# A new instruction order for an S4 block with an MLP: the MLP's first four column blocks computed in two halves of the tokens

## The chip, the core and the metric

The kernel runs on one core of a Trainium2 chip. The core has five engines that run on their own and meet through semaphores: TensorE (PE; its weight loads are shown apart as PEld), VectorE (DVE), ScalarE (ACT), GpSimd (POOL) and SyncE (SP), which only issues DMAs here. Matrix products land in PSUM, eight banks per partition; everything else lies in SBUF. The metric is the device time of one execution in microseconds, as the median over runs.

## What is computed

The input x has 2048 tokens of 512 channels (bf16). First a state-space convolution is added to it, then an MLP:

```python
h  = x + A(layernorm(x))          # y = irfft(rfft(u) * rfft(K)) + u * Dskip, per channel, 2048 taps
h2 = h + B(layernorm(h))          # B: layernorm, gelu(y @ w1 + b1) @ w2 + b2; w1 is 512 x 1376
# the taps, from 128 complex modes per channel:
K[d, l] = Re( sum_n C[d,n] * exp(dt[d] * A[d,n] * l) * dt[d] * B[d,n] )
# l is rounded to bf16 before the exponential
```

## The kernel before

The convolution is done with a Fourier transform of 4096 points split into two factors, on PE. Channels are handled in four groups c = 0 to 3 of 128; tokens in two halves b = 0 and 1, each of two quarters sb. The stages, with the lines that do them:

1. Loads and small tables. The decay th = dt * A_re comes from an exponential on ACT, a transpose on PE and one DVE product (L791). From it ACT makes exponentials (`bexps`, L795 and L798; `aexps`, L1016). Other DVE work builds phases (`split`, `wrap`, `restack`). A table load (`table`, L557) switches ACT from exponentials to sines.
2. `chain` (four calls): PE adds phases in PSUM (L1062, L1068), ACT takes sine and cosine (L1072), DVE multiplies them with the exponentials (L1039, L1079 to L1090). In the calls of kind "B" the sine table is negated in place (L1080, "sign pass") between two uses.
3. `kgen` (per channel group): 512 small matmuls in two lines (L1113, L1114) give the taps of a group; ACT or DVE casts them out of PSUM (`evac`: L563 on ACT, L565 on DVE), and a small DVE addition (L1127) puts in Dskip. `carry` (L1134) shifts rows with four DMAs of SP.
4. `kspec` (L1157), a write to DRAM (`AK_d`) and a read back turn the layout; `fstage` (L989) finishes the kernel's spectrum. This is done for each pair of channel groups q and each block.
5. `xspec` (L969) and `fstage` do the same for the input, after layer norm (`ustats`, `stats`, `unorm`).
6. `inverse` (per b and c): DVE or GpSimd multiplies spectra (L1205, L1210, L1213), PE transforms back (L1221), `evac` casts, and a transposing DMA of SP (`turn`, L1227) puts tokens on partitions.
7. `lead` and `tail`: adding the convolution to x, statistics, a reciprocal root on GpSimd (`root`, L925), scale and shift (L1340 on ACT or L1338 on DVE), and the transpose of the normalized tokens, on PE for the first quarter (L1349, cast at L1351) and by `turn` for the others.
8. `mlp` (per quarter): 11 column blocks of w1, four matmuls of 512 tokens each (L1369), gelu on ACT (L1371), and the second product (L1391) with the addition of h on DVE (L1393) and the store.

Nothing is scheduled while the kernel runs. Each `add` call makes one operation and numbers it, in program order, from 0 to 969. The list ORDER, written out in the file, is the order in which the operations are emitted, and each engine does its own in that order. A negative entry ~n means operation n on the second engine of those that it allows. `Sched.run` walks the list with planned costs and arrival times; the plan decides which of four PSUM tiles of two banks an operation gets (`slots`) and where PE gets filling matmuls (L1485) in planned gaps. Operations of GpSimd wait for the DVE operation that stands before them in the list ("turns").

Operations that matter below, by their numbers in the old list:

| numbers | what |
|---|---|
| 15; 16 to 18 | bit fields: GpSimd's memsets; three DVE operations on them (L695 to L697) |
| 47, 48 | th and its negative copy |
| 76 to 79 | two DVE sums and their squares on ACT |
| 108, 116 | the scaled copies of `split` |
| 545 to 552 | statistics of the input's second half (L945) |
| 418 to 433; 434 | `kgen` of groups 2 and 3; its last cast |
| 436 to 439; 440, 443 | `carry` and `kspec` for groups 2 and 3, first block |
| 446, 447; 448, 449 | writes of that spectrum to DRAM; reads back |
| 408, 409 | reads of the second block of groups 0 and 1 |
| 450 to 457; 469 to 476 | `fstage` and casts, first and second block of groups 2 and 3 |
| 534, 538, 541; 542, 543 | last products of the first half's inverse; its last transform and cast |
| 544 | the `turn` of it |
| 575 to 608 | parts of `xspec(1)` and their casts |
| 609 to 615 | loads of w1 (four, 344 KB each), w2 (two of 640 KB, one of 96 KB) |
| 639; 640 | `root` of the first quarter; scale and shift from it |
| 641, 643, 646, 648 | the normalizations of the first quarter's four token tiles |
| 645, 650 | the casts of the two halves of its transpose |
| 674 to 694 | the MLP's column blocks of the first quarter (even numbers PE, odd ones ACT; 694 is the last) |
| 727 to 776; 777 | products of the second half's inverse; its last transform |

Of the kernel before, what the change touches and what calls it, by code (L numbers as in the profile page):

```python
# [162 lines left out]
class VS(V):  # L163
# [91 lines left out]
class Ring:  # L255
# [12 lines left out]
    def until(self, t0):  # L268
        o = 0.0
        for a, b in self.q:  # L270
            o += max(0.0, min(b, t0 + 5.0) - max(a, t0))
        return t0 + 3.3 + 0.4 * min(o, 5.0)


class Sched:
# [40 lines left out]
    def run(self, nslots):  # L316
# [13 lines left out]
        for code in ORDER:  # L330
# [46 lines left out]
            if e == "PE":  # L377
# [4 lines left out]
                while n0 < ipe:  # L382
# [3 lines left out]
                    if (n1 - 193) % 256 == 0:  # L386
                        t = blk = max(t, ring.until(blk))
# [39 lines left out]
def c_dve(n, mode=1, psum=False):  # L427
    return (0.09 if n < 64 else 0.065) + (0.07 if psum and n > 700 else 0) + n / mode / 960.0
# [1098 lines left out]
```

## Time and profile before

| | us |
|---|---|
| median of three runs | 240.29 (240.02 to 241.02) |
| the profiled execution | 238.53 |
| its span, first to last instruction | 236.8 |
| PE busy | 203.2 (86%) |
| DVE busy | 176.7 (75%) |
| ACT busy | 172.2 (73%) |
| GpSimd busy | 46.0 (19%) |
| mean granted clock of PE | 0.990 |

Times in the profile count from the first instruction. Busy time says little here, since the stages have different limits: a stage is read by which engine is nearly full in it, and by the chain of waits, which goes back from the last instruction to what released it each time. "issue" in that chain is time in which the engine waited for nothing that the profile shows. L12 is line 12 of the kernel. A group's time may be a helper's: all casts have L563 or L565.

### The profile page before, as it was taken

What the parts mean: (1) busy time and instruction counts of PE and PEld (TensorE: products, weight loads), DVE (VectorE), ACT (ScalarE), POOL (GpSimd) and SP (SyncE); (2) the same over time, 40 slices, a digit from 0 to 9 for tenths busy, and PEclk for the clock granted to TensorE, in tenths of its full rate; (3) what the DMA queues carried; (4) which work ended last, traced back from release to release, by engine and by line L of the source; (5) the groups of instructions that cost most, each with busy time, mean ns of one, the idle gap of its engine ahead of it and who ended that gap; (6) DMA issues with size and microseconds to landing.
All of it is one profiled execution on the core that took longest, in us unless ns stands there. A gap on an engine that the chain in (4) does not pass through costs nothing.

```text
span 236.8 us, 7706 instructions
## 1 busy us (share of the span) xinstructions
PE 203.2 (86%) x3285; PEld 114.0 (48%) x3285; DVE 176.7 (75%) x323; ACT 172.2 (73%) x210; POOL 46.0 (19%) x224
## 2 busy tenths in 40 slices
PE   3219686768999999998979888999999999999994
PEld 2203432324875387865657544544444444444443
DVE  3999997999999975678979999988954757222022
ACT  5999999899899996696979959989456305604700
POOL 5945760000000140319400001520000101000000
PEclk9999999997999999999999999999999999999998
DMA  5692210200000549534897797470654051421212
GB/s 172 145 202 60 60 36 0 48 2 3 6 3 10 136 126 278 200 93 143 250 233 160 174 220 202 112 178 24 121 110 83 0 111 44 91 55 48 51 33 55
DMA packets 42293, 24.15 MB, mean 102 GB/s; under 512 B 25810, under 2 KB 39604, under 8 KB 42260
## 3 DMA queue, kind: packets, MB, share of 16 engines
q1 hardware_dynamic: 41810, 23.34, 41.2%
q8 instruction: 25, 0.41, 0.7%
q10 hardware_dynamic: 450, 0.33, 0.6%
q14 instruction: 8, 0.07, 0.1%
HBM read 9.90 MB, written 6.29 MB: 68 GB/s over the span
## 4 chain that ended last, share of the span: by engine, by line
PE 53%; ACT 24%; DMA 8%; DVE 7%; issue 5%; SPq 1%; POOL 1%; DVEq 0%; ACTq 0%; POOLq 0%
PE ps L1369 16%; PE ps L1391 13%; ACT ar L798 6%; ACT ar L563 6%; PE ps L1114 4%; PE ps L1113 4%; ACT ar L1072 4%; ACT ar L1016 4%; DMA ar<-ar 4%; PE ps L1068 3%; PE ps L969 3%; DMA ar<-AK_d 3%; PE ps L989 2%; ACT ar L647 2%; PE ps L1157 2%
## 5 line engine op out<-in xcount | busy, mean ns | idle before, releaser
L563 ACT CAST ar<-ps 128x1024 bf16<-128x1024 f32 (+4 forms) x72 | 65.1, 970 | 16.7 <-PE ps L1287 2.8
L1371 ACT ACTIVATE ar<-ps,ar 128x512 bf16<-128x512 f32 (+1 forms) x44 | 28.8, 688 | 30.9 <-PE ps L1369 29.7
L1369 PE MATMUL ps<-ar 128*128 128x512 bf16 (+1 forms) x176 | 40.2, 379 | 0.3 <-ACT ar L563 0.3
L1391 PE MATMUL ps<-ar 128*128 128x512 bf16 (+3 forms) x187 | 39.9, 367 | 0.0
L1072 ACT ACTIVATE ar<-ps 128x1024 bf16<-128x1024 int16 x36 | 34.7, 1049 | 1.9 <-PE ps L1068 1.6
L1393 DVE TENSOR_TENSOR ar<-ps,ar 128x512 bf16<-128x512 f32 (+1 forms) x17 | 11.2, 658 | 28.9 <-PE ps L1391 24.2
L565 DVE CAST ar<-ps 128x1024 bf16<-128x1024 f32 (+1 forms) x20 | 23.3, 1185 | 8.8 <-PE ps L1114 3.7
L1205 DVE TENSOR_TENSOR ar<-ar 128x2048 bf16<-128x2048 bf16 x21 | 25.2, 1220 | 3.6 <-PE ps L1221 3.3
L1391 PEld LDWEIGHTS <-ar 128*128 128x128 bf16 (+1 forms) x187 | 17.9, 98 | 19.8 <-issue 0.4
L1369 PEld LDWEIGHTS <-ar 128*128 128x128 bf16 (+1 forms) x176 | 17.3, 100 | 20.6 <-issue 1.1
L1068 PE MATMUL ps<-ar 128*32 128x512 f16 (+1 forms) x368 | 21.8, 346 | 5.6 <-ACT ar L1072 5.6
L1485 PE MATMUL ps<-ar 128*128 128x512 bf16 x57 | 15.7, 412 | 9.3 <-DMA ar<-in_A_u_dram 7.2
L1114 PE MATMUL ps<-ar 128*20 128x33 bf16 x512 | 20.9, 249 | 1.2 <-issue 1.2
L1113 PE MATMUL ps<-ar 128*20 128x33 bf16 x512 | 20.7, 248 | 0.5 <-issue 0.4
L925 POOL TENSOR_TENSOR ar<-ar 128x4 f32<-128x4 f32 (+1 forms) x5 | 5.7, 1148 | 77.8 <-DVE ar L614 51.5
L1113 PEld LDWEIGHTS <-ar 128*20 128x20 bf16 x512 | 18.5, 124 | 2.2 <-issue 1.3
L989 PE MATMUL ps<-ar 128*32 128x256 bf16 (+1 forms) x384 | 18.9, 310 | 0.6 <-DMA ar<-AK_d 0.3
L1114 PEld LDWEIGHTS <-ar 128*20 128x20 bf16 x512 | 18.3, 125 | 2.1 <-issue 1.7
L1068 PEld LDWEIGHTS <-ar 128*32 128x32 f16 x368 | 10.3, 101 | 15.2 <-issue 12.4
L969 PE MATMUL ps<-ar 128*32 128x512 bf16 x256 | 17.0, 380 | 0.6 <-issue 0.5
L1039 DVE TENSOR_TENSOR ar<-ar 128x2048 bf16<-128x2048 bf16 x14 | 16.5, 1212 | 0.0
L624 DVE TENSOR_TENSOR ar<-ar 128x4 f32<-128x4 f32 (+8 forms) x38 | 12.9, 352 | 3.7 <-POOL ar L693 2.8
(113 smaller groups left out, 289.4 us busy)
## 6 DMA issues: line engine op xcount, KB each, us to landing
AK_d<-ar SPq DMA_DIRECT2D x8, 512.0 KB
ar<-AK_d SPq DMA_DIRECT2D x8, 512.0 KB
ar<-in_A_u_dram SPq DMA_DIRECT2D x4, 512.0 KB
out_dram<-ar SPq DMA_DIRECT2D x30, 64.0 KB
ar<-in_B_w_dram SPq DMA_DIRECT2D x4, 344.0 KB
ar<-ar SPq DMA_DIRECT2D x20, 64.0 KB
ar<-in_B_w_dram SPq DMA_DIRECT2D x2, 640.0 KB
ar<-ar SPq DMA_DIRECT2D x8, 48.0 KB
```

The source lines that it names most:

```text
L563: act.copy(out_fn(), in_fn())
L565: dve.tensor_copy(out_fn(), in_fn())
L969: pe.matmul(pst(p)[32 * cg:32 * cg + 32, 512 * z:512 * z + 512], lhsT=BD.ap()[:, 32 * f + 2 - 2 * jl:32 * f + 34 - 2 * jl], rhs=un[2 * (2 ...
L989: pe.matmul(pst(p)[64 * h + z:64 * h + z + 32, w * (k + r):w * (k + r) + w], lhsT=T.ap()[:, f, r, z:z + 32], rhs=rhs(f), start=True, stop= ...
L1068: pe.matmul(pst(p)[32 * g:32 * g + 32, 256 * j:256 * (j + n)].rearrange("p (a b) -> p a b", a=n), lhsT=W2[DELTAS.index(d)].ap(), rhs=S2[g] ...
L1072: add("ACT", c_act(1024), lambda e, o_=o_, i_=i_: act.activation(o_(), i_(), ACT.Sin, scale=SINSC), r=[p, TBL], w=[sc[cs]])
L1113: pe.matmul(o, lhsT=Ar.ap()[:, :, d], rhs=Br.ap()[:, :, d], start=True, stop=False, tile_position=(0, 32 * g))
L1114: pe.matmul(o, lhsT=Ai.ap()[:, :, d], rhs=Bi.ap()[:, :, d], start=False, stop=True, tile_position=(0, 32 * g))
L1205: (dve if e == "DVE" else gp).tensor_tensor(pieces(o).rearrange("p z (a r d) -> p a z r d", a=4, r=2), k, x, ALU.mult)
L1369: pe.matmul(pst(p)[:fs, 512 * z:512 * z + 512], lhsT=w1s[dc].ap()[:, fc * P:fc * P + fs], rhs=ybuf.ap().rearrange("p (t c) k -> p c t k", ...
L1371: add("ACT", c_act(512, 1), lambda e, p=p, z=z, fc=fc, fs=fs: act.activation(hT.ap()[:fs, fc, :], pst(p)[:fs, 512 * z:512 * z + 512], ACT. ...
L1391: pe.matmul(pst(p)[:, 512 * z + c0:512 * z + c1], lhsT=hT.ap()[:fs, fc, 128 * t:128 * t + 128], rhs=w2s[fc].ap()[:fs, c0:c1], start=(fc == ...
```

## The change

There are four parts.

- `mlp`: for the first quarter of the tokens and the first four column blocks, the four matmuls over 512 tokens become two operations of four matmuls over 256 tokens each. The first reads only the first half of the transposed input. This makes four operations more, 974 in all; numbers above 674 shift by up to four in the new file. The text goes on with the old numbers.
- The sign pass may be put on GpSimd by the list, and its instruction has two constants, -1 and 1.
- ORDER is another list. Operations change their place in every queue, and some fifty their engine.
- The planner's constants differ: when PE's instructions are refilled (`Ring.until`, 192 for 193), the costs of the first loads, of transposes on PE.
- Nothing else changes: the same products, tables and transfers.

```diff
@@ ORDER (beginning, and the stretch from the first casts to the MLP)
-    163, -204, 0, 81, 1, 11, 12, 43, 44, 15, 132, 16, 17, 18, 2, 45, 5, 162, 3, 131, 6, 161, 66, 4, 14, 13, 46, 47, 50, 48, 62, 34, 19, 8, 60, 54, 28,
...
+    43, -27, 81, -287, 82, 131, 12, 0, 44, 1, 11, 46, -204, 4, 14, 2, 38, 132, 15, 3, 67, 45, 47, 13, 48, 5, 16, 17, 68, 66, 49, 18, 50, 87, 69, 163,
...
+    276, 418, 419, 420, 423, 386, 503, 545, 421, 546, 383, 504, 402, 547, 548, 403, 422, 549, 404, 161, 424, 425, 550, 551, 552, 553, 554, 427, 428,
+    483, 501, 405, 502, 406, 484, 507, 555, 508, 556, 426, 429, 430, 558, 557, 432, 433, 485, 505, 559, -280, 388, 560, 561, -279, -432, 387, -563,
...
+    490, 511, 396, 611, 491, 439, 578, 579, 580, 438, 437, 436, 443, -513, 444, 446, 509, 498, 499, 510, -446, 615, 409, 397, 398, -501, 572, 573,
+    574, -619, 280, 599, 600, 515, -517, 524, 590, 591, 592, 518, 519, 520, 416, 417, 527, 408, 412, 410, 411, 569, 570, -572, 413, 525, 528, 529,
+    521, 447, -726, 448, 450, 449, 452, -527, -452, 595, 522, 453, -597, 610, 456, 457, 454, 455, 575, 531, 576, 534, 577, 538, 458, 532, 535, 460,
+    533, 530, 597, 541, 536, 593, 598, -595, 523, 724, 726, 727, 539, 540, 542, 543, 739, 459, 414, 415, 584, 537, 585, 587, 588, 589, 619, 620, 623,
+    728, 729, 624, 730, -587, -733, 461, 462, 621, 622, 626, 464, 625, 463, 544, 651, 627, 652, 654, 628, 629, 653, 603, 604, 631, 630, 581, 582, 583,
+    632, 634, 605, 612, 465, 633, 606, 656, 635, 636, 659, 637, 601, 466, 638, 639, 602, 607, 608, 655, 657, 640, -647, -642, -644, 609, 642, 658,
...
@@ Ring
     def until(self, t0):
         o = 0.0
         for a, b in self.q:
-            o += max(0.0, min(b, t0 + 5.0) - max(a, t0))
-        return t0 + 3.3 + 0.4 * min(o, 5.0)
+            o += max(0.0, min(b, t0 + 5.5) - max(a, t0))
+        return t0 + 3.65 + 0.3 * min(o, 5.5)
@@ chain
-                add("DVE", c_dve(1024, 4), lambda e, sc=sc: dve.tensor_scalar(sc[0].ap(), sc[0].ap(), -1.0, None, ALU.mult), r=[sc[0]], w=[sc[0]])
+                add(("DVE", "POOL"), (c_dve(1024, 4), 0.92), lambda e, sc=sc: (dve if e == "DVE" else gp).tensor_scalar(sc[0].ap(), sc[0].ap(), -1.0, 1.0, ALU.mult, ALU.mult), r=[sc[0]], w=[sc[0]], hv=9)
@@ mlp
-                def fn(e, p=p, z=z, fc=fc, fs=fs):
-                    for dc in range(4):
-                        pe.matmul(pst(p)[:fs, 512 * z:512 * z + 512], lhsT=w1s[dc].ap()[:, fc * P:fc * P + fs], rhs=ybuf.ap().rearrange("p (t c) k -> p c t k", c=4)[:, dc], start=(dc == 0), stop=(dc == 3))
-                add("PE", 0.87, fn, r=[ybuf] + w1s, w=[p], new=[p] if z == 0 else [], hv=1)
+                for t0, t1 in ((0, 2), (2, 4)) if b + sb == 0 and fc < 4 else ((0, 4),):
+                    def fn(e, p=p, z=z, fc=fc, fs=fs, t0=t0, t1=t1):
+                        for dc in range(4):
+                            pe.matmul(pst(p)[:fs, 512 * z + 128 * t0:512 * z + 128 * t1], lhsT=w1s[dc].ap()[:, fc * P:fc * P + fs], rhs=ybuf.ap().rearrange("p (t c) k -> p c t k", c=4)[:, dc, t0:t1], start=(dc == 0), stop=(dc == 3))
+                    add("PE", 0.2175 * (t1 - t0), fn, r=[ybuf[4 * t0:4 * t1]] + w1s, w=[p], new=[p] if z == 0 and t0 == 0 else [], hv=1)
```

More of the change, by code (lines that the diff above doesn't have):

```diff
@@ L382, in run @@
                 while n0 < ipe:
-                    n1 = min(ipe, n0 - (n0 - 193) % 256 + 256)
+                    n1 = min(ipe, n0 - (n0 - 192) % 256 + 256)
                     t = clk.work(t, c * (n1 - n0) / o.ni, o.act / o.cost[0])
                     n0 = n1
-                    if (n1 - 193) % 256 == 0:
+                    if (n1 - 192) % 256 == 0:
                         t = blk = max(t, ring.until(blk))
@@ L655 @@
     tE(bf16, 512)
-    dma("ACT", lambda: ldt.ap(), lambda: A_log_dt.rearrange("(o d) -> o d", o=1), 1024, [], [ldt], pr=0, cost=0.42)
+    dma("ACT", lambda: ldt.ap(), lambda: A_log_dt.rearrange("(o d) -> o d", o=1), 1024, [], [ldt], pr=0, cost=-0.28)
     for n, (nm, ap) in enumerate((("are", A_A_re), ("cre", A_C_re), ("cim", A_C_im), ("bre", A_B_re), ("bim", A_B_im), ("aim", A_A_im))):
         raw[nm] = tE(bf16, 4, P)
-        dma(("SP", "ACT", "SP", "ACT", "SP", "SP")[n], lambda v=raw[nm]: v.ap(), lambda a=ap: a.rearrange("(p dt) n -> p dt n", dt=4), 131072, [], [raw[nm]], pr=0.01 * n, cost=0.42)
+        dma(("SP", "ACT", "SP", "ACT", "SP", "SP")[n], lambda v=raw[nm]: v.ap(), lambda a=ap: a.rearrange("(p dt) n -> p dt n", dt=4), 131072, [], [raw[nm]], pr=0.01 * n, cost=(0.0, 0.05, 0.42, 0.05, 0.42, 0.42)[n], k=1.25)
     xv = x_dram.rearrange("(b q j h l) d -> b h q j (l d)", b=2, j=4, h=2, l=2)
@@ L785, in fn @@
                 pe.transpose(pst(p, bf16)[:, 128 * d:128 * d + 128], raw[nm].ap()[:, d, :], identb.ap())
-        add("PE", 0.6, fn, r=[raw[nm], identb], w=[p], new=[p])
+        add("PE", 0.3, fn, r=[raw[nm], identb], w=[p], new=[p])
         return p, (lambda: nat(pst(p, bf16)[:, 0:512]))
@@ L812, in trf @@
                 pe.transpose(pst(p, bf16)[:, 512 * n + 128 * d:512 * n + 128 * d + 128], raw[nm].ap()[:, d, :], identb.ap())
-        add("PE", 0.6, trf, r=[raw[nm], identb], w=[p], new=[p] if n == 0 else [])
+        add("PE", 0.27, trf, r=[raw[nm], identb], w=[p], new=[p] if n == 0 else [])
         pas.append(lambda p=p, n=n: nat(pst(p, bf16)[:, 512 * n:512 * n + 512]))
```

57 rows, old and new, of the table ORDER are left out of this document.

## The prediction

> **What bounds the kernel now.** I first read the span, the bandwidth in 40 slices of 5.9 us, and a table of busy times by stage (columns: length, then PE, its weight loads, DVE, ACT and GpSimd, each with its number of instructions; granted clock; busy share of the DMA engines; GB/s), with stages cut where the chain of waits changes hands.
>
> ```profile
> span 236.8 us, 7706 instructions
> ...
> GB/s 172 145 202 60 60 36 0 48 2 3 6 3 10 136 126 278 200 93 143 250 233 160 174 220 202 112 178 24 121 110 83 0 111 44 91 55 48 51 33 55
> ...
> 36.30:83.60 47.30, 39.74 (x1019) 23.63 (x1017) 45.86 (x92) 44.05 (x52) 0.80 (x3) 0.96 0.12 26
> 83.70:101.90 18.20, 16.78 (x661) 14.16 (x657) 10.90 (x18) 13.37 (x14) 4.31 (x4) 1.00 0.62 196
> 101.90:120.70 18.80, 17.89 (x413) 11.11 (x403) 17.02 (x17) 16.70 (x19) 9.37 (x4) 1.00 0.67 188
> 120.70:135.40 14.70, 12.66 (x313) 8.96 (x313) 12.84 (x13) 12.97 (x14) 0.00 (x0) 1.00 0.87 164
> 135.40:150.00 14.60, 13.02 (x145) 6.67 (x145) 13.58 (x29) 10.99 (x15) 1.03 (x1) 1.00 0.94 229
> 150.00:173.50 23.50, 23.44 (x187) 10.95 (x186) 22.10 (x37) 17.28 (x24) 5.08 (x2) 1.00 0.47 102
> ...
> 195.20:236.80 41.60, 38.06 (x188) 18.27 (x185) 11.72 (x26) 14.47 (x22) 1.01 (x1) 0.98 0.23 54
> ```
>
> From 36 to 84 us DVE is busy for 45.86 of 47.30 us; from 84 to 102 PE is (16.78 of 18.20), from 102 to 150 nobody alone, and from 150 on PE is busy throughout. So the end is the time at which the MLP's PE work begins, plus what PE still has to do, plus its waits. Then the chain of waits (start, length, what), in order of time.
>
> ```profile
> 4.02 0.18 DVE ar L624
> ...
> 4.78 0.64 DVE ar L624
> 5.44 0.63 ACT ar L795
> 6.07 8.52 ACT ar L798 x9
> 14.59 1.04 ACT ar L647 x2
> ...
> 18.14 0.52 ACT ar L632
> ...
> 23.15 0.52 ACT ar L632
> ...
> 34.54 1.28 ACT L557
> ...
> 88.08 0.43 PE ps L989 x8
> ...
> 101.96 0.51 DVE ar L565
> ...
> 114.65 6.03 DMA ar<-AK_d
> ...
> 122.72 1.24 issue
> ...
> 128.81 4.74 ACT ar L563 x5
> ...
> 135.40 5.46 DMA ar<-ar
> ...
> 142.48 1.30 ACT ar L563 x2
> ...
> 145.93 2.21 ACT ar L1340 x3
> 148.14 0.51 ACT ar L563
> ...
> 148.94 1.02 ACT ar L563
> 150.00 1.94 PE ps L1369 x8
> ...
> 172.75 0.77 DVE ar L1213 x2
> 173.56 0.56 PE ps L1221 x14
> ...
> 195.21 9.50 PE ps L1369 x44
> ```
>
> The reader should see five hand-overs: a late start of ACT (5.44); PE until the kernel of the last channels is out (101.96); a round trip through DRAM until 120.68; ACT's casts until 135.4; the transposing DMA, statistics and normalization until 150.0. Last, the grouping by line gives prices (busy, mean ns of one, idle before):
>
> ```profile
> L1205 DVE TENSOR_TENSOR ar<-ar 128x2048 bf16<-128x2048 bf16 x21 | 25.2, 1220 | 3.6 <-PE ps L1221 3.3 <-ACT ar L563 0.2
> ...
> L1205 POOL TENSOR_TENSOR ar<-ar 128x2048 bf16<-128x2048 bf16 x3 | 12.2, 4069 | 13.3 <-DMA ar<-ar 8.2 <-ACT ar L563 5.1
> ...
> L945 DVE BATCH_NORM_STATS2 ar<-ar 128x6 f32<-128x512 bf16 x16 | 9.7, 670 | 0.0
> ...
> L1080 DVE TENSOR_SCALAR ar<-ar 128x1024 bf16<-128x1024 bf16 x8 | 3.3, 426 | 0.0
> ...
> L1434 DVE TENSOR_SCALAR ar<-ar 128x1024 bf16<-128x1024 bf16 x1 | 0.4, 443 | 0.0
> ```
>
> **The change part by part.** Numbers of operations are those of the old list. The planner's new constants move no operation of the list; they set only how many filling matmuls (L1485) are put into planned gaps of PE, which wait for nothing and are costed at 0, and which PSUM tile an operation gets.
>
> *The sign pass* (L1080) gets a second engine, but no negative entry of the new list names one of its eight operations: it stays on DVE. Its new two-constant form is that of L1434, 443 ns against 426: 8 x 0.02 = +0.1, taken as 0.
>
> *The split* adds 16 matmuls and 16 weight loads. Only one half block (674, first half) stands in the new list ahead of work that needs both halves of the transposed input: after it come 732, then 694 with all tokens. That is 0.43 us of PE work (two matmuls' worth at 9.50/44 = 0.216) and the 0.47 of 732, in the gap between the two casts at 148.14 and 148.94, where the old list had 469 and 471 (2 x 0.43). So I take 0 (ends: -0.4, and +0.4 if weight loads show between short matmuls).
>
> *The order* is the rest. Step 1: the first product (47, row 4.78) stood behind three field operations that waited for GpSimd (4.02 on). Now 47 and 48 stand first. The timeline has 47's two inputs, the exponential and the transpose:
>
> ```profile
> 2.65 0.60 ACT L647 ACTIVATE ar<-ps 128x512 bf16<-128x512 f32 x1
> ...
> 2.94 0.61 PE L785 MATMUL ps<-ar 128*128 128x128 bf16 x4 [0.33 <-DMA ar<-in_A_A_re_dram]
> ```
>
> Both were ready at 3.6, so 47 starts at 3.7 and ACT 1.0 earlier. GpSimd's identity, now behind five memsets of DVE (some 0.7 us), is hidden by the load that this transpose waits for. Step 2: two scaled copies (rows 18.14, 23.15) leave ACT for DVE, 2 x 0.52 = -1.0. But ACT now reaches the squares (row 14.59) at 4.4 + 2 x 0.52 + 7 x 0.947 (8.52/9) = 12.1, and DVE has their inputs at some 13.6 only, one earlier than before: +1.0. Together -1.0 at the table load (34.54).
>
> Step 3, the DVE stage to 83.6: eight statistics (545 to 552; 9.7/16 = 0.6 each from start to start) go behind it, -4.8 with what hangs on them -5.7, and 3.9 of small work, most of it from GpSimd, comes in. The last product would be 2.8 earlier with step 1. But PE now does one kernel-spectrum group and four input groups ahead of 418, which the old list had behind, and gets there at some 83. I take -1.0 for 418 (ends 0, -2.8).
>
> Step 4, PE to 101.96: ten groups of eight matmuls leave the stretch up to 433, at 0.43 each (row 88.08): -4.3. Their casts have room (ACT 13.37 and DVE 10.90 of 18.20). The last kernel cast is 5.3 earlier, at 96.7.
>
> Step 5, the round trip (carry, spectrum, write 447, read 448 and 449; 18.7 us in the rows from 101.96 to 120.68). SP's timeline has the writes 446 and 447 (start, length from the first issue to the end of the last):
>
> ```profile
> 106.59 4.30 SPq L575 DMA_DIRECT2D AK_d<-ar  x2
> ```
>
> SP's queue now has 615 (96 KB) and the reads 409 and 408 (512 KB each) between 446 (512 KB) and 447. That is 1.6 MB ahead of 447, 6.5 us at 250 GB/s (the fastest slices from 89 to 124 us show 278, 250 and 233), of which 4.3 pass before 447 is issued anyway: +2.2. Arrival at 117.6, 3.1 earlier.
>
> Step 6, arrival to the last cast of the first inverse (543), 14.7 us: ACT has nine casts left after the first PE group (457, 455, 577, 460, 533, 536, 598, 540, 543), 0.7 + 9 x 0.95 (4.74/5) = 9.2, where thirteen and three waits stood. DVE's three products behind the second of them end earlier than that. So -5.5: 543 ends at 126.8, 8.6 earlier.
>
> Step 7, to the MLP: the transposing DMA (5.46) and the statistics stay. ACT then has five postponed casts (604, 583, 606, 602, 608) before the first normalization, 0.4 + 4.7 us from the last lead cast's start, where 3.4 passed (142.48 to 145.93): +1.7. One normalization more on ACT is balanced by PE starting on the first of two casts. GpSimd's root (639) stands behind a 4.07 us product, which starts eight DVE operations earlier. The weights 609 are moved from 90.5 to behind write 466, whose casts stand ten casts ahead of 650 on ACT; a load of 344 KB lands in that time. So far 6.9 earlier, 143.1.
>
> How tight is that? From 83.7 to 150.0 ACT is busy 13.37 + 16.70 + 12.97 + 10.99 = 54.0 of 66.3 us, idle 12.3. The new list gives ACT 2.0 more in that stretch (counted at 0.9 a cast) and the steps make it 5.8 shorter: 4.5 idle of 60. Its densest stage above has 44.05 of 47.30, the same share. I give back 1.1, the ends being 0 and all 6.9: the MLP begins at 144.2, and the scale and shift that release the normalizations (640) are 5.8 earlier.
>
> Step 8, after the MLP began. PE has 1.8 more to do (469, 471, 732, 740 follow instead of preceding). DVE has more, too: four products' worth of the second half (727, 729, 736, 737 and four small ones, 5.9) came behind 640, four tail operations (2.4) went ahead, and one product comes from GpSimd (1.1; another went there earlier): +4.3 net of a normalization. DVE's timeline has 640 at
>
> ```profile
> 145.57 0.16 DVE L640 SCALAR_TENSOR_TENSOR ar<-ar 128x4 f32<-128x4 f32 x1
> ```
>
> From there to the last product (172.75 + 0.77 = 173.52) DVE took 27.9; now 32.2, from 139.8 to 172.0. PE comes to that inverse (777) after 25.0 us (48 matmuls of L1369 and 44 of L1391 at 0.216 take 19.9, six inverse groups at 0.56 3.4, four spectrum groups at 0.43 1.7), at 169.2, and waits 2.9. Its work from there on is 0.65 shorter. The end moves by (172.1 - 173.56) - 0.65 = -2.1 us. Most of the early gain is given back here.
>
> The profiled execution took 238.53 us for a span of 236.8, 1.8 below the median of 240.29; a difference of spans is put on the median: 238.2.
>
> In the Trainium skill, Runtime: NRT & Kernel Launch, section Instruction fetch mechanics, refills of 256 instructions are called mostly hidden. Its rule prices the 32 added PE instructions at nothing, which is the sum above. The row 122.72 disagrees, if that wait is a refill: PE waited 1.24 us for nothing that the profile shows while DMA was 0.87 busy. With one more such wait the sum would be 239.4.
>
> **The rivals.** *No change*: DVE decides. If 640 comes only 3.7 earlier, step 8 returns all of it: -3.7 + 4.3 - 0.65 = 0, 240.3. For it: 22.10 of 23.50 us busy on DVE after 150. Against: 1.4 idle there may also close.
>
> *Slower*: the round trip of step 5. The stage 120.7 to 135.4 moved 164 GB/s at 0.87 busy; at that rate the 1.6 MB take 9.9 us, 3.4 later, and the end is +1.3: there it decides. At 150 GB/s it is +4.4 on the arrival, +2.3, 242.6. For it: 408 and 409 now fall into the trip; before, 447 had the queue to itself. Against: the stage 135.4 to 150.0 moved 229.
>
> *The order doesn't bring the MLP forward*: a list is matched to planned durations, and what is gained up to 433 goes into waits between five queues in fixed order. With 640 where it was, step 8 alone is left: +4.3 - 0.65 = +3.6, 243.9. For it: idle time of 4.5 us in 60 is little for ACT. Against: ten groups out of the stretch that PE bounds is a count and no plan.
>
> **How the numbers follow.** Forecast -2.1: 0.53, from 234.6 (-2.1, less the 1.1 given back, step 3's other 1.8 and half of DVE's 1.4 idle) to 239.1. No change, 239.1 to 241.5: 0.20. Slower by the round trip, 241.5 to 243.5: 0.17; by an MLP that isn't earlier, 242 to 245: 0.10. The range leaves out about 0.1 on each side: 234.5 to 243.0. 0.5% is 1.2 us, about what a measurement can tell. So faster 0.53, same 0.20, slower 0.27.
>
> **What would show it.** Steps 1 and 2: first L795 at 4.4, second table load at 33.5. Step 4: the last L1127 at 97. Step 5: the first inverse group after the read at 118. Step 7: first L1369 near 144. Step 8: PE idle before one L1221 group, released by L1213, near 170. I am wrong if the read lands after 121, if L1369 starts after 147, or if PE does not wait there at all (then faster still).

## The result, and the profile after

The changed kernel is slower: 242.19 us median (240.08 to 243.02) against 240.02 us of the kernel before, measured beside it; ratio 1.0124, 95% interval 1.0078 to 1.0171. The forecast was 238.2 us, faster. The same kernel was timed three more times beside the experiments, on three chips, at ratios of 1.0048 (1.0005 to 1.0090), 1.0062 (1.0018 to 1.0106) and 1.0039 (0.9998 to 1.0080). So it loses 0.4 to 1.2%, and the sign of the forecast was wrong. The profiled execution after took 240.91 us for a span of 239.1, before 238.53 for 236.8. Line numbers of the changed kernel are one higher than before up to L1367, two higher behind the MLP's matmul, which was L1369 and is L1371.

First the page's span of the changed kernel and its table of busy times by stage, cut where the same operations end that cut the table before (columns as there).

```profile
span 239.1 us, 7770 instructions
...
82.20:100.40 18.20, 14.70 (x594) 12.10 (x596) 9.12 (x21) 11.75 (x12) 1.92 (x3) 0.91 0.51 155
100.40:121.40 21.00, 19.87 (x473) 12.38 (x464) 17.85 (x21) 18.49 (x20) 10.00 (x5) 1.00 0.73 203
121.40:131.30 9.90, 9.62 (x244) 6.59 (x245) 9.27 (x9) 8.83 (x10) 0.35 (x1) 1.00 1.15 153
131.30:148.40 17.10, 16.30 (x184) 7.46 (x182) 14.91 (x33) 16.15 (x21) 5.10 (x2) 1.00 0.85 237
148.40:176.10 27.70, 26.78 (x270) 14.59 (x273) 26.16 (x38) 20.18 (x27) 1.01 (x1) 1.00 0.47 101
```

The kernel stage (first row, from 418 to 433) begins 1.5 us earlier and has 2.1 us less PE work than before (14.70 for 16.78), and yet it is as long (18.20). Its mean granted clock is 0.91, where it was 1.00. The stage behind it (the DRAM round trip) is 2.2 longer, the next one 4.8 shorter, the one to the MLP 2.5 longer. Then the chain of waits (start, length, what), first three rows of the kernel before, then the changed kernel.

```profile
88.89 0.36 issue
...
96.71 0.55 issue
...
224.58 8.69 PE ps L1391 x51
```

```profile
90.08 1.82 issue
...
96.98 1.39 issue
...
107.12 1.03 PE ps L1158 x16
108.25 1.24 DVE ar L566
109.53 6.04 DMA AK_d<-ar
115.95 5.48 DMA ar<-AK_d
121.47 0.65 PE ps L990 x16
...
131.67 1.02 ACT ar L564
...
148.44 0.60 PE ps L1371 x4
...
226.94 8.69 PE ps L1393 x51
```

The reader should see two things. Two waits for nothing that the profile shows, 1.82 and 1.39 us, stand in the kernel stage, where the longest was 0.55 before. And the MLP begins at 148.44, 1.6 earlier than before, but the last PE row ends at 235.63, where it ended at 224.58 + 8.69 = 233.27. So 3.9 us are lost behind the MLP's beginning. Most of it is PE's own work, as the busy times from there to PE's end show (columns as above), before and after:

```profile
150.00:233.27 83.27, 83.14 (x491) 38.90 (x490) 45.35 (x87) 40.72 (x58) 7.09 (x4) 1.00 0.33 70
```

```profile
148.44:235.63 87.19, 86.10 (x567) 41.95 (x572) 48.56 (x87) 43.80 (x62) 3.02 (x3) 1.00 0.34 72
```

PE is busy 3.0 us longer (0.4 of it two filling matmuls) and idle 1.0 us longer. DVE's timeline has the two ends that the forecast used for this part, the scale and shift (640) and the last product of the second half's inverse (776, second of the two in its row).

```profile
143.75 0.16 DVE L641 SCALAR_TENSOR_TENSOR ar<-ar 128x4 f32<-128x4 f32 x1
...
175.18 0.76 DVE L1214 TENSOR_TENSOR ar<-ar 128x512 bf16<-128x512 bf16 x2
```

From 143.75 to 175.94 it is 32.2 us. Before it was 27.9, and 32.2 was forecast.

The milestones of the runs that follow, read from the traces (us; 433 is the last kernel matmul group, 447 the last spectrum write, 456 the first group of `fstage` after the read, 543 the last cast of the first inverse; "MLP" is the first MLP matmul, "rest" the time from it to PE's end):

```
run              433 ends  447 issued  456 starts  543 ends  640    MLP     rest
before            101.9      110.5       120.7      135.4   145.6  150.0    83.3
changed           100.4      109.5       121.5      131.2   143.8  148.4    87.2
changed, 2nd      100.2      109.3       120.3      129.8   142.6  147.3    87.2
changed, 3rd      100.2      110.3       122.8      132.1   144.9  149.6    87.2
changed, 4th      100.4      110.4       122.6      131.9   144.6  149.3    87.2
old_list          103.2      111.5       121.9      135.3   145.3  149.8    83.3
old_new_543       102.5      111.0       122.1      135.6   146.4  151.8    87.2
thin               96.7      105.8       116.9      126.9   139.1  143.8    87.2
late_387           97.9      110.0       120.3      129.7   142.5  147.2    87.2
```

The last column is the key to the result. In every trace of this table the new order needs 3.9 us more than the old one from the MLP's first matmul to the end. Only the beginning of the MLP moves from run to run. The change is faster than before when that beginning is over 3.9 us earlier, and it is 0.4 to 2.7 earlier in the changed kernel's four traces. The end of 433 alone doesn't set that beginning: in old_list 433 ended 1.3 us later than before and the read came 1.2 later, but 543 and the MLP did not, so the old order has that much room behind its read.

### The profile page after: what moved, and what is told of

It is laid out like the page before. It is cut to its first block, busy times and chain, and to the rows that moved or that the text cites. A ratio compares the mean times of both kernels' runs of the same rounds, so it can differ in the third digit from the quotient of the medians.

```text
span 239.1 us, 7770 instructions
## 1 busy us (share of the span) xinstructions
PE 209.4 (88%) x3317; PEld 116.8 (49%) x3331; DVE 175.9 (74%) x328; ACT 175.3 (73%) x213; POOL 41.5 (17%) x216
## 4 chain that ended last, share of the span: by engine, by line
PE 54%; DVE 19%; ACT 12%; DMA 6%; issue 4%; POOL 3%; SPq 1%; POOLq 0%; DVEq 0%
PE ps L1393 16%; PE ps L1371 15%; DVE ar L1040 5%; ACT ar L564 4%; PE ps L1114 4%; PE ps L1115 3%; PE ps L990 3%; ACT ar L1017 3%; DVE ar L625 3%; DMA AK_d<-ar 3%; DMA ar<-AK_d 2%; PE ps L1158 2%; PE ps L970 2%; PE ps L1069 2%; DVE ar L641 2%
## 5 line engine op out<-in xcount | busy, mean ns | idle before, releaser
L564 ACT CAST ar<-ps 128x1024 bf16<-128x1024 f32 (+4 forms) x75 | 67.9, 970 | 14.9 <-PE ps L990 7.3
L1371 PE MATMUL ps<-ar 128*128 128x512 bf16 (+2 forms) x192 | 40.7, 362 | 0.6 <-ACT ar L564 0.3
L1073 ACT ACTIVATE ar<-ps 128x1024 bf16<-128x1024 int16 x36 | 34.5, 1051 | 2.6 <-PE ps L1069 2.5
L1487 PE MATMUL ps<-ar 128*128 128x512 bf16 x79 | 22.3, 411 | 9.3 <-DMA ar<-in_A_u_dram 8.5
L1371 PEld LDWEIGHTS <-ar 128*128 128x128 bf16 (+1 forms) x192 | 18.7, 100 | 20.1 <-issue 2.2
L1393 PEld LDWEIGHTS <-ar 128*128 128x128 bf16 (+1 forms) x187 | 17.9, 98 | 20.0 <-issue 1.0
L566 DVE CAST ar<-ps 128x1024 bf16<-128x1024 f32 (+2 forms) x17 | 19.4, 1161 | 9.9 <-PE ps L1115 6.7
L1114 PE MATMUL ps<-ar 128*20 128x33 bf16 x512 | 20.1, 249 | 3.4 <-issue 3.2
L1069 PE MATMUL ps<-ar 128*32 128x256 f16 (+1 forms) x368 | 20.3, 330 | 1.6 <-ACT ar L1073 1.6
L1115 PE MATMUL ps<-ar 128*20 128x33 bf16 x512 | 20.6, 248 | 1.0 <-issue 1.0
L1115 PEld LDWEIGHTS <-ar 128*20 128x20 bf16 x512 | 18.0, 124 | 4.0 <-issue 3.7
L990 PE MATMUL ps<-ar 128*32 128x256 bf16 (+1 forms) x384 | 18.6, 319 | 1.3 <-DMA ar<-AK_d 1.2
L1114 PEld LDWEIGHTS <-ar 128*20 128x20 bf16 x512 | 18.1, 124 | 2.9 <-issue 1.4
L1487 PEld LDWEIGHTS <-ar 128*128 128x128 bf16 x87 | 8.1, 103 | 22.0 <-issue 16.0
L970 PE MATMUL ps<-ar 128*32 128x512 bf16 x256 | 17.5, 395 | 0.0
L1040 DVE TENSOR_TENSOR ar<-ar 128x2048 bf16<-128x2048 bf16 x14 | 16.7, 1215 | 0.3 <-POOL ar L615 0.3
L1206 POOL TENSOR_TENSOR ar<-ar 128x2048 bf16<-128x2048 bf16 x3 | 12.2, 4069 | 21.7 <-PE ps L1222 14.7
```

Source lines behind the costliest of these rows:

```text
L564: act.copy(out_fn(), in_fn())
L990: pe.matmul(pst(p)[64 * h + z:64 * h + z + 32, w * (k + r):w * (k + r) + w], lhsT=T.ap()[:, f, r, z:z + 32], rhs=rhs(f), start=True, stop= ...
L1040: dve.tensor_tensor(o, E_(o).unsqueeze(1).to_broadcast(shape), f, ALU.mult)
L1069: pe.matmul(pst(p)[32 * g:32 * g + 32, 256 * j:256 * (j + n)].rearrange("p (a b) -> p a b", a=n), lhsT=W2[DELTAS.index(d)].ap(), rhs=S2[g] ...
L1073: add("ACT", c_act(1024), lambda e, o_=o_, i_=i_: act.activation(o_(), i_(), ACT.Sin, scale=SINSC), r=[p, TBL], w=[sc[cs]])
L1114: pe.matmul(o, lhsT=Ar.ap()[:, :, d], rhs=Br.ap()[:, :, d], start=True, stop=False, tile_position=(0, 32 * g))
```

## The experiments

**The order, not the split.** The expectations speak of three theories. A: the front of the new order gains and its back, behind 640, loses. B: the front itself loses, by refills of PE's instructions and by the half clock. C: the split, the filling matmuls or the PSUM tiles cost something. Two kernels take the change apart: the old order in the changed program, and the new order without the split.

```diff
 # old_list: the changed program, the old list with the new numbers
-ORDER = [the new list]
+ORDER = [the old list, the two halves of a block behind each other]
 # no_split: the new list, one operation for a block, where its second half stood
-for t0, t1 in ((0, 2), (2, 4)) if b + sb == 0 and fc < 4 else ((0, 4),):
+for t0, t1 in ((0, 4),):
```

> Everything of the change but the order: the split, the two-constant sign pass and the planner's constants, with the operations in the old list's order (the two halves of a block follow each other). If the order is the cause (theories A and B): the same time as before, ratio 0.997 to 1.004. If the split or the moved filling matmuls and PSUM tiles cost something (theory C): 1.005 to 1.012.

> The new order without the split: each of the four blocks is one operation again, at the place of its second half. If the order is the cause (A and B): as slow as the changed kernel, ratio to before 1.008 to 1.016. If the split is (C): 0.997 to 1.004.

The old list in the changed program ran at 239.02 us, ratio 1.0011 (0.9974 to 1.0047): the split, the sign pass and the constants cost nothing that can be measured. Without the split the new order had 240.33 us, ratio 1.0040 (1.0007 to 1.0073), where the expectation began at 1.008. The unedited changed kernel, timed again (below), gave the same: the loss is smaller than the first measurement said, and it is the order's. The intervals of the times overlap; what separates the orders is the column "rest", 83.3 with the old list in the changed program and 87.2 with the new one.

**Front and back of the order.** Two splices take one list up to an operation and the other list for all that is left then. The second was repeated one operation later.

```diff
 # old_new_543: the old order up to 543, then the new one; new_old_543: the reverse
+ORDER = OLD[:n] + [c for c in NEW if c not in OLD[:n]]
 # new_old_544: the reverse, spliced at the turn 544
+ORDER = NEW[:n] + [c for c in OLD if c not in NEW[:n]]
```

> The other way round: the old order up to operation 543, the new order for what is left. Theory A: 543 ends near 135.4 as before, the scale and shift (640) come no earlier than before or up to 2 us later, and DVE's work behind them is longer than before by up to 4 us: the end is 2 to 6 us later, ratio 1.008 to 1.025. Theory B: as before, 0.996 to 1.004.

> The new order up to the last cast of the first inverse (operation 543, the cast that ends 135.38 before and 131.24 after), the old order for all that is left then. Theory A: the front of the new order is a gain of 4 us at that cast, which its back part gives away by DVE's 4.3 us behind 640; with the old back the first MLP matmul is 2 to 4 us earlier than before and the end 1.5 to 3.5 us, ratio 0.985 to 0.994. Theory B (the front loses: refills and the half clock are what makes the change slower): no better than before, 1.000 to 1.010.

> The new order up to the issue of the first transposing DMA (operation 544), the old order after it. In the splice at 543 a write to DRAM that the old order has early (466) stood ahead of 544 on SP and waited for casts that the new front has late: 544 went out 9.5 us after its input. With the splice one step later this is gone. Theory A (loss behind 640): 544 is issued near 131.3 (before 135.4), 640 runs at 142 to 143.5 (145.6), from there to the last product of the first inverse pair (776) 27.9 us as before, not 32.2; ratio 0.985 to 0.995. Theory B (the front is no gain): 0.998 to 1.010.

The old front with the new back ran at 244.37 us, ratio 1.0243 (1.0190 to 1.0296). DVE's timeline of it:

```profile
146.36 0.16 DVE L641 SCALAR_TENSOR_TENSOR ar<-ar 128x4 f32<-128x4 f32 x1
...
178.54 0.76 DVE L1214 TENSOR_TENSOR ar<-ar 128x512 bf16<-128x512 bf16 x2
```

640 is 0.8 later than before, and from there to the last product it is 32.9 us. PE's rest is 87.2 us, 3.9 more than before. This is the loss of the new back, alone: the half of theory A that concerns the back holds, though by PE's work more than by DVE's.

The reverse failed twice: 247.35 us, ratio 1.0368 (1.0323 to 1.0412), and 247.96, ratio 1.0341 (1.0250 to 1.0433). The second has the turn 544 at 131.35, as expected, but the scale and shift only at 153.95. PE's timeline of that run shows why (L1487 is the filling matmul, which stands where PE was planned to wait):

```profile
140.54 1.89 PE L1487 MATMUL ps<-ar 128*128 128x512 bf16 x8 [0.30 <-ACT ar L564]
142.37 0.62 PE L990 MATMUL ps<-ar 128*32 128x512 bf16 x8
142.92 4.71 PE L1487 MATMUL ps<-ar 128*128 128x512 bf16 x21
147.56 0.62 PE L1222 MATMUL ps<-ar 64*128 64x128 bf16 x16
148.11 0.23 PE L1284 MATMUL ps<-ar 128*128 128x128 bf16 x1
```

The new front reaches 543 early because five casts and their PE groups are put off. In the old order those stand ahead of an inverse group (732, the L1222 row), and that stands ahead of the lead's matmuls (L1284, L1288), whose last cast (629) the changed kernel has at 139.5 and this one at 149.8. So the 4.1 us at 543 are not a gain that the old order could keep; as far as this splice shows, they are in good part work put off. Theory A was wrong in that half.

**What holds the kernel stage.** PE's waits by what was waited for (total, times, longest), before and after; the two lines of the kernel matmuls are L1113 and L1114 before, L1114 and L1115 after:

```profile
PE ps L1114 <- issue: 1.2, 3, 0.6
...
PE ps L1113 <- issue: 0.4, 1, 0.4
```

```profile
PE ps L1114 <- issue: 3.2, 2, 1.8
...
PE ps L1115 <- issue: 1.0, 3, 0.5
```

In the trace the longer waits of this kind stand 256 instructions of PE apart, or a multiple of it (within one record): before at PE's records 1980, 2236, 3004, 3260, 3516, 3772 and 4796, after at 1720, 3255 and 3511. The page of the changed kernel lists an instruction queue with 26 packets of 16 KB in all, and in the kernel stage a packet lands 1.2 to 1.6 us ahead of the end of each wait. The packets of that stage, from the trace's DMA records (us):

```
                before                         changed
packet starts   86.12  90.66  94.22  98.64     84.41  89.59  95.92  99.48
lands           87.86  91.59  95.70  99.75     85.41  90.47  96.86  100.41
PE goes on      89.26  92.98  97.26  100.99    86.80  91.90  98.37  101.82
```

Where no transfer runs (61 to 76 us), the packets of both kernels mostly start 3.4 to 3.8 us apart. In the changed kernel there are 5.2 and 6.3 us between them. From 85.7 to 89.5 two writes of 512 KB are in flight there, from 91.5 a third write and 1 MB of reads. Theory R: a refill of PE's instructions that falls due while bulk transfers are in flight starts late. The rival: the refills have their own pace, or the low clock holds PE. One kernel puts 1 MB of writes where nothing runs in the kernel before, one leaves most of 2 MB out of the changed kernel (some 1.8 MB), one leaves the same out before.

```diff
 # bulk: the kernel before, with two writes more
     unorm(0, 3.4)
+    bulk = [dram.tile([8, P, 256], bf16, name=f"bulk{n}") for n in range(2)]
+    for n in range(2):
+        dma("SP", lambda n=n: bulk[n].rearrange("z p c -> p z c"),
+            lambda: UN[0][0].ap()[:, :256].unsqueeze(1).to_broadcast([P, 8, 256]), 524288, ...)
 # thin, thin_before: kstage writes nk of 8 rows and reads np of 128 partitions
+        nb, nk, np = (len(bs), 1, 8) if D is AK_d[0][0] else (len(bs), 8, P)
```

> The kernel before with 1 MB more written to DRAM in packets of 512 bytes, 61 to 66 us, where PE takes 256 instructions in 3.2 to 3.7 us and no transfer runs. Nothing reads what is written. If transfers in flight delay the refill of PE's instructions (theory R), the 16 KB packet that starts at 64.8 before starts 1.5 to 3.5 us later and PE waits 1.5 to 3 us for nothing that the profile shows near 67.5 (0.14 before). If the refill has its own way, its packet starts within 0.3 us of the time before and takes at most 1.7 us.

> The changed kernel with the writes and reads of the first channels' first kernel spectrum (387, 388, 389, 390; 2 MB) cut to an eighth of the rows and an eighth or less of the partitions, so that its output isn't the reference's. Read only for the stretch from the first kernel matmul of the last channels (418) to the last (433). Theory R (the refills are late because these transfers are in flight): the two waits of 1.8 and 1.4 us shrink to 0.6 or less, and 433 ends 2.5 to 4 us earlier than 100.4, at 96.5 to 98. If the refills' own pace (3.4 to 3.7 us for 256 instructions) is what holds PE, or the half clock, 433 ends within 1 us of 100.4.

> The same cut in the kernel before. Its five refills in this stretch are 3.8 us apart on average, 3.45 without transfers, so theory R leaves little to gain: 433 ends 1 to 1.8 us earlier than 101.9. Against the run with the changed kernel it shows what the groups taken out of the stretch are worth once the refills are free: 1.5 us if 256 instructions in 3.45 us set the pace (112 instructions less), 3.0 if PE's own work does (7 groups at 0.43).

The run with 1 MB more, in SP's timeline and in PE's:

```profile
61.83 1.10 SPq L575 DMA_DIRECT2D bulk<-ar  x2
```

```profile
69.34 0.27 PE L1113 MATMUL ps<-ar 128*20 128x33 bf16 x4 [1.96 <-issue]
```

The packet that started at 64.84 before now started at 67.06, and PE waited 1.96 us where it had waited 0.14. So bulk writes can hold a refill up: this execution shows it, at a place that has nothing else to do with the change.

With the 1.8 MB left out of the changed kernel (a single execution, 236.24 us beside 238.38 for the kernel before), PE's waits, the chain of waits and DVE's timeline:

```profile
PE ps L1114 <- issue: 0.7, 2, 0.5
```

```profile
105.75 5.59 DMA AK_d<-ar
111.35 4.02 DMA ar<-AK_d
...
143.78 0.60 PE ps L1371 x4
```

```profile
139.09 0.16 DVE L641 SCALAR_TENSOR_TENSOR ar<-ar 128x4 f32<-128x4 f32 x1
...
170.51 0.76 DVE L1214 TENSOR_TENSOR ar<-ar 128x512 bf16<-128x512 bf16 x2
```

433 ends at 96.7, 3.8 earlier than in the changed kernel, and theory R holds for it. The forecast had the last kernel cast at 96.7, the MLP at 144.2 and the end 2.1 us earlier than before; here the cast starts at 96.8, the MLP at 143.8, and the time is 2.1 less. With the refills undisturbed, and 1.8 MB less to move, the forecast comes out, though, as the section below shows, not all for its reason.

The same cut in the kernel before did the opposite of the expectation: 433 ended at 103.6, 1.7 later. Its waits, and its clock beside the longest of them (columns of the table by stage):

```profile
PE ps L1114 <- issue: 2.3, 2, 1.9
```

```profile
98.40:101.60 3.20, 3.20 (x77) 2.63 (x81) 0.00 (x0) 0.77 (x1) 0.00 (x0) 0.50 0.02 5
```

With the writes gone, other reads (609 and 408, issued at 90.2 and 90.6) met a refill: PE went on at 92.67, the packet due then started at 95.81 and landed at 96.76. So the old order is not free of this: with it, PE also waited 1.42 us in old_list and 1.97 in old_new_543 at the last refill of the stretch, where it waited 0.32 in the kernel before. And transfers in flight don't always hold a refill up. The packets of 90.66 and 94.22 in the kernel before started 1.40 and 1.24 us after PE had gone on, little later than the 1.1 where no transfer runs, with the DMA engines 0.78 and 1.03 busy in the microsecond ahead. Theory R is therefore half a rule: what decides whether a packet gets through stays open.

**Can the new order have its refills back with all the work done?** Two kernels move writes on SP, and nothing else.

```diff
 # SP's queue, old numbers: late_387, then late_writes
-406, 388, 387, 407, 389, 390, 611, ...
+406, 388, 407, 387, 389, 390, 611, ...
+406, 407, 388, 387, 389, 390, 611, ...
```

> The changed kernel with one write of the first channels' kernel spectrum (387, 512 KB) behind the write 407 on SP; nothing is left out. Then only 512 KB are in flight when PE, from 86.8 on, needs its next instructions, and 1 MB starts near 91.7, as the refill after it is due. Theory R: the first wait (1.8 us near 90.1) shrinks to 0.7 or less, the second to 1.5 or less, the clock stays full, and the last kernel matmul (433) ends 1.5 to 3.5 us earlier than 100.4; the reads behind are issued 3 to 5 us later than 91.2 and land near 102, in time for their users at 103.5. The end is 1 to 3 us earlier than the changed kernel's, ratio to before 0.994 to 1.003. If the refills' own pace or the half clock alone set the stretch, 433 ends within 1 us of 100.4 and the time is the changed kernel's.

> The same with both writes (388 and 387) behind 407. Nothing is in flight at the refill after 86.8; 1.5 MB start near 91.7. Theory R: the first wait shrinks to 0.6 or less, the second to 1.5 or less; 433 ends 1.5 to 3.5 us earlier than 100.4. The reads are issued near 98 and land near 103, up to 2 us late for their users: ratio to before 0.996 to 1.006.

> The changed kernel unedited beside them: ratio to before 1.004 to 1.012, two waits of over 1 us between 418 and 433.

Both ended 433 earlier, at 97.9 and 96.4, and their clock in the kernel stage stayed full. The busy times from 418 to 433 (columns as in the table by stage) in late_writes and in the changed kernel's fourth trace show that PE's work is the same, and that only its waits differ, 0.6 and 5.0 us:

```profile
82.62:96.37 13.75, 13.15 (x594) 11.79 (x596) 9.18 (x21) 10.92 (x12) 1.97 (x3) 1.00 0.35 104
```

```profile
82.22:100.40 18.18, 13.16 (x591) 11.78 (x593) 9.10 (x21) 11.36 (x12) 1.96 (x3) 0.98 0.51 154
```

Neither kept it: 239.61 us, ratio 1.0050 (1.0021 to 1.0078), and 242.44, ratio 1.0149 (1.0095 to 1.0203), against 240.13, ratio 1.0039, for the changed kernel beside them. Between late_387 and the changed kernel no difference can be told: the median is lower, the ratio higher, and the intervals overlap. SP's timeline and PE's chain of late_387:

```profile
98.22 0.81 SPq L576 DMA_DIRECT2D ar<-AK_d  x2
...
109.98 0.37 SPq L576 DMA_DIRECT2D AK_d<-ar  x1
```

```profile
101.07 1.83 PE ps L1487 x8
102.90 0.55 PE ps L990 x16
...
107.57 0.97 PE ps L1158 x16
```

The reads that had run from 91.2 are issued at 98.2 now, and PE fills 1.83 us until the `fstage` groups that need them (L990). The spectrum group ahead of 447 (L1158) ends at 108.54, in the changed kernel at 108.15, so all of the 2.5 us is gone at that point. In late_writes the reads are issued at 99.3, and that group ends at 110.1. In these two orders the transfers have no free place: ahead of 433 they hold up the refills, behind it the data.

**The round trip.** The three transfers between the last two writes were moved.

```diff
 # sp_trip: SP's queue, old numbers
-389, 390, 611, 439, 438, 437, 436, 446, 615, 409, 408, 447, 448, 449, ...
+389, 390, 409, 408, 611, 439, 438, 437, 436, 446, 447, 448, 449, 615, ...
```

> The changed kernel with SP's three transfers taken out from between the last two spectrum writes: the load 615 behind the reads, the reads 409 and 408 ahead of the load 611 (SP is idle from 92.8 to 100.4). If those 1.1 MB delay the round trip, the last read is issued 3.4 us after its write's issue (113 or so) instead of 6.1, and the first inverse group runs 2 us earlier, near 119.5; with DVE deciding from there, the end is 1 to 2 us earlier than the changed kernel's: ratio to before 1.000 to 1.006. If the reads take time that is free, no difference to the changed kernel. If transfers in flight hold up the refills of PE's instructions, the reads now fall on the refill at 95.9 and eat part of it: the last kernel matmul (433) ends 0.5 to 2 us later than 100.4.

> The changed kernel once more, unedited, to stand beside the others on one chip. Both theories: ratio to before 1.008 to 1.017 as measured first. If the split is a cause (theory C), it stands clearly above the kernel without the split (1.004) and above 1.008; if the order alone is, it lies at 1.003 to 1.008.

```profile
91.58 3.79 SPq L576 DMA_DIRECT2D ar<-AK_d  x4
...
105.81 7.01 SPq L576 DMA_DIRECT2D AK_d<-ar  x2
115.72 0.81 SPq L576 DMA_DIRECT2D ar<-AK_d  x2
```

From the last write's issue (112.44, inside the second row) to the read's it is 3.3 us, as before the change, and 6.1 in the changed kernel: the mechanism is right. But the write itself comes 2.9 us later, and the kernel ran at 242.57 us, ratio 1.0161 (1.0077 to 1.0245), beside 1.0048 for the changed one. 433 ends at 100.3, no later than in the changed kernel. Of the 2.9 us, 1.7 have passed by the next input group (L970, at 104.33 for 102.58), where a stretch at half the clock (99.73 to 103.15) and a refill wait of 0.63 lie; the other 1.2 are filling matmuls, for a wait that was planned. Whether the moved megabyte brought these about was not tested.

**DVE behind 640.** One product went back to GpSimd.

```diff
 # pool750
-... 750 on DVE ...
+... 750 on GpSimd, as in the old list ...
```

> The changed kernel with one product (750) back on GpSimd, where the old list has it. If DVE's work from the scale and shift (640) to the last product of that inverse pair (776) decides, it takes 31.0 us, not 32.2, PE's group 777 starts 1.2 us earlier, and the kernel is 0.8 to 1.2 us faster than the changed one beside it. If PE's work decides there, the same time within 0.4 us.

> The changed kernel unedited beside the one with the product on GpSimd. Ratio to before 1.004 to 1.012; 640 to 776 takes 32.2 us, 418 to 433 17 to 18 us with two waits of over 1 us.

It ran at 242.86 us, ratio 1.0188 (1.0144 to 1.0232), beside 240.13, ratio 1.0062, for the changed kernel. 640 to 776 took 34.5 us: 2.3 longer instead of 1.2 shorter. GpSimd's timeline and DVE's:

```profile
151.42 4.07 POOL L1206 TENSOR_TENSOR ar<-ar 128x2048 bf16<-128x2048 bf16 x1 [9.32 <-DVE ar L1214]
```

```profile
152.37 4.20 DVE L1206 TENSOR_TENSOR ar<-ar 128x2048 bf16<-128x2048 bf16 x1 [1.09 <-PE ps L1222]
```

DVE's own product (1.22 us elsewhere) took 4.20 while GpSimd's ran. The Trainium skill, SBUF — State Buffer, section Who interferes with whom, says that a DVE instruction with two SBUF inputs contends with a GpSimd instruction that reads SBUF; this trace agrees, at 3 us for one product. PE's rest grew by the same 2.3 us (89.5 for 87.2), so DVE's length behind 640 does set the end there, in the direction not expected. In the changed kernel it hardly does: PE has its other work done at 175.70 and the last product ends at 175.94, so a shorter DVE alone could have gained PE 0.2 us, and 0.4 with the two filling matmuls that stand there.

## Why the prediction was wrong

Its sum was: MLP 5.8 earlier, 3.7 given back behind it. Measured: 1.6 earlier, 3.9 given back.

- **Steps 1 and 2 were right.** ACT starts the first exponential at 4.40 (4.4 forecast), and the second table load is at 33.83 (33.5 forecast; it was 34.54).
- **Step 3 was right.** 418 starts 1.55 us earlier (1.0 forecast, ends 0 and 2.8). The last of the five products that it needs ends 1.55 earlier, too (81.99 for 83.54), and PE comes from its spectrum group 0.2 us behind it, so both arrive together, where the forecast had PE as the later one.
- **Step 4 failed, and it is nearly the whole error: 3.9 of 4.5 us (2.1 earlier forecast for PE's end, 2.4 later measured).** It took ten groups at 0.43 us off the stretch to 433, -4.3, because PE was busy for 16.78 of 18.20 us, and it let PE's waits stay as they were. 433 came 1.4 earlier (5.3 forecast), no more than 418 did: from 418 to 433 it is 18.2 us, for 18.1 before. PE's work in the stretch did fall. Seven of the groups left it (the others had stood ahead of 418), 112 instructions of 1280, and at full clock PE is busy for 13.2 us, where it was 16.7. But PE's waits grew, from 1.4 us before to 5.0 in the fourth trace; in the first they are 3.5, and the half clock makes the 13.2 into 14.7. What step 4 overlooked is in the trace before: four waits in that stretch, 256 instructions of PE apart, and packets of 16 KB 3.5 to 4.5 us apart. The kernel matmuls are short (80 instructions in some 0.7 us), so PE runs through 256 of them in some 2.1 us, less than the 3.4 to 3.8 between packets where nothing else runs, and each refill that is late holds it up. In the changed kernel two were late, with transfers in flight. With the transfers cut the stretch took 14.4 us, and 13.8 in late_writes, 3.7 and 4.3 less than before: the groups were worth about what step 4 gave for them, as long as no refill came late. Whether PE's work or the pace of the refills (four crossed in the stretch, where it was five) sets those 13.8 us was not separated.
- **The Trainium skill's rule on refills was weighed at the wrong place.** The Trainium skill, Runtime: NRT & Kernel Launch, section Instruction fetch mechanics, calls a refill mostly hidden. The trace disagrees where PE's instructions are short: 1.82 and 1.39 us of waiting here, 1.96 in the run with 1 MB more. I used the rule for the 32 instructions added in the MLP, where the packets are 8.6 us and more apart and it holds, and did not ask it of the kernel stage. The row 122.72, which the prediction took for a refill on a condition, is one: it stands 1024 instructions behind the wait before it, and a packet lands at 122.69, 1.28 us ahead of its end.
- **Step 5 was right in mechanism and 0.4 us short:** from the write 447 to the read it is 6.1 us for 3.4, +2.6 (2.2 forecast). The arrival is 0.7 later than before instead of 3.1 earlier, the difference being step 4's.
- **Step 6 was right:** from arrival to 543 it is 9.8 us for 14.7, -4.9 (5.5 forecast).
- **Step 7 was right:** from 543 to the MLP 17.2 us for 14.6, +2.6 (1.7 and 1.1 given back, 2.8 forecast).
- **Step 8 was right in the sum by luck.** 640 to 776 takes 32.2 us, as forecast to the tenth. Its wait was wrong: PE does not wait 2.9 us near 170 for DVE. It arrives at 175.7, 0.2 ahead of the product's end, after waits of some 0.9 us for ACT's casts and gelu, and has some 2.5 us more to do than before where I counted 1.8 less 0.65. The give-back is 3.9 us all the same (3.7 forecast), but it is PE's work and ACT's casts.

Of the rivals, "no change" had the gain ahead of 640 given back behind it, which is what came, with 1.8 us gained at 640 where it needed 3.7. "The order doesn't bring the MLP forward" had its reason, gains that go into waits, but 640 did come earlier; its 243.9 is above what was measured. "Slower by the round trip" named transfers that are in the way, which is what happened, but one stage earlier than it said and to PE's refills.

The half clock is a companion of the waits, and where it falls decides whether it costs. The stretch of 3.4 us with the lowest clock, in the changed kernel and in its fourth run:

```profile
92.40:95.80 3.40, 3.40 (x56) 2.14 (x49) 0.54 (x2) 1.01 (x1) 0.00 (x0) 0.52 0.95 242
```

```profile
99.40:102.80 3.40, 3.40 (x79) 1.77 (x73) 2.86 (x8) 1.46 (x2) 0.76 (x1) 0.54 0.39 112
```

In the first it lies inside the stretch that refills hold, the wait behind it is 1.39 us, and 433 ends at 100.4. In the fourth the clock is full there, the wait is 3.22, and 433 ends at 100.4: what the slow clock took, PE would have waited. But then the slow stretch comes behind 433, where PE has work, and the write 447 goes out at 110.4 instead of 109.5. The first two traces have it early and their MLP at 148.4 and 147.3, the third and fourth late and theirs at 149.6 and 149.3. The kernel pool750, which is the changed one as far as the MLP, has no slow stretch in its trace: there 447 goes out 9.1 us behind the end of 433, as in the first two, where the third and fourth take 10.0. (Its 433 ended at 99.2, as its packet of 94.87 was less late.) So the slow stretch costs some 1.0 us behind 433; no experiment set the clock itself.

## What to carry to other kernels

In this kernel a busy share of 92% didn't make the engine the bound: look whether its short waits stand a fixed number of instructions apart, and if they do, ask of each what will be in flight when it falls due, since a piece that is removed can come back as a longer wait. The stage with many short matmuls lost by bulk transfers, and when one is moved, ask both what it passes and what will wait for it: here each place that freed the refills made data late. When an order is replaced, sum each engine's work behind the milestone too, PE's first where it is busy for 83.1 of 83.3 us; the 3.9 us that were moved behind the MLP's beginning came back in full, in every trace of the table that has the new back.

## What the runs showed of the hardware

- With transfers in flight, a 16 KB instruction packet of the changed kernel started 4.0 us after PE had gone on (91.90 to 95.92), where it is 1.1 without them: 2.9 us late. 1 MB of added writes made PE wait 1.96 us, while the packet itself took 0.9 to 1.7 us. Two packets of the kernel before started 1.40 and 1.24 us after, with the DMA engines 0.78 and 1.03 busy, so transfers in flight alone don't decide it.
- In the changed kernel's four traces and in the thinned kernel before, 3.4 us at half the clock (0.50) began beside a wait of 1.8 to 3.2 us among these short matmuls, between 0.2 us ahead of the wait's end and 1.4 behind it; waits up to 1.57 us had none. Yet the wait of 1.96 us with 1 MB more written had a full clock behind it, and so had one of 1.97 in old_new_543, so the length of a wait alone doesn't decide. The Trainium skill, TensorE: Matmul & The Clock Gate, section What's actually happening, has the clock set by how busy PE was in freely running windows of some 3.4 us; the length of the slow stretches agrees.
- One product on GpSimd made DVE's product 3.4 times as long (4.20 us), so moving it to DVE, as the change did, was a gain in the new order: PE's rest is 87.2 us with it and 89.5 without.
